# Turning six experts' token tiles by DMA: 16-bit planes stored by ScalarE and DMA transposes, for TensorE transposes

## The chip, the cores and the metric

The kernel runs on one core of a Trainium2 chip, alone. A core has engines that work from their own instruction queues: TensorE (PE, with its weight loads PEld), VectorE (DVE), ScalarE (ACT), GpSimd (POOL) and SyncE (SP), which here only issues DMAs. The metric is the device time of one execution in microseconds; a kernel is told by the median of its runs. Numbers of parts come from one profiled execution.

## The reference

Attention with a soft cap, and then a mixture of eight experts over its output. The routing is greedy and global: the largest logits first, each token to one expert, each expert at most 448 of the 3584 tokens.

```python
scores = cap * np.tanh(scale * np.matmul(q, k.transpose(0, 1, 3, 2)) / cap)
attn = softmax(scores);  x = attn @ v                # 8 x 12 heads, 448 x 64
x = x.transpose(0, 2, 1, 3).reshape(3584, 768)
flat = (x @ w_gate).flatten()
for idx in np.argsort(-flat):                        # token idx//8, expert idx%8
    if assigned[token] >= 0 or counts[e] >= 448: continue
    assigned[token] = e; counts[e] += 1
for e in range(8):
    h = np.maximum(x[mask_e] @ w1[e], 0.0)           # 448x768 @ 768x1024
    out[mask_e] = h @ w2[e]                          # 448x1024 @ 1024x768
```

All is float32. The products of the experts are made of pairs of rounded parts (a high part and the rest), three products for one.

## The kernel before, in words

The first 370 us are attention; it writes its output x, 3584 rows of 768, to a DRAM tensor `xs`. From 380 us on the experts follow each other, p = 0 to 7 in the code (expert one to expert eight in the text).

**One expert.** The first layer `ffn1` has eight steps f of 18 matmuls (144), the second layer `ffn2` eight units u: token tiles t = 0, 1, 2 of 128 tokens with 24 matmuls each and t = 3 of 64 tokens with 16, for each half of the 768 columns (176 matmuls). After every matmul the program calls `tick()`. The count of these ticks is the program's clock: at fixed ticks it writes other work into the engines' queues. PE, ACT, DVE and POOL run what the program has written, in that order; a queue's instruction starts when the queue comes to it and its semaphores allow it.

**The tokens of the next expert.** While expert p is in its second layer, the routing (class `Routing`) ends the choice of the tokens of expert p+1: `finalise` leaves the row numbers (`idx`) and the expert's number (`ei`) at tick 39 of the second layer. At tick 40 `gather(p+1)` issues four indirect DMAs on POOL (line 782): rows of `xs`, 3 KB each, to the tile `xg`, tokens on partitions. The first layer needs x the other way round, features on partitions. `xtr(p+1, c)` does this for one of six chunks c of 128 features: four TensorE transposes (line 798) to a PSUM tile psX, then `cutx`: ACT copies the rounded high part to `xgh` (line 803), DVE subtracts for the low part `xgl` (line 804). For expert p of 1 and above the six chunks lie in units u = 5, 6, 7 (the table CP); for expert two they lie in units 6 and 7 of expert one and in the first step of its own first layer (the table CL and the work lists).

**The routing beside it.** From tick 79 of the second layer on, the routing searches thresholds for expert p+2: steps of seven comparisons, five on DVE (line 503) and two on ACT (line 500, `cmpA`), whose counts a small matmul (line 507, psR) sums up. The psR matmuls stand between the matmuls of the second layer at fixed ticks: 94, 110, 126, 139, 159. The last search is that of expert seven, so it runs beside the second layers of experts two to five and not beside those of six and seven.

**Weights.** The tiles w1r (384 KB, four buffers) and w2r (768 KB, four buffers) are loaded by SP (lines 743 and 750), whose queue runs ahead of the ticks until a buffer is not free or the expert's number is not known (line 734). ACT rounds them to high parts (line 755), POOL subtracts for the low parts (line 759): `split1` and `split2`. Each finished PSUM tile of the second layer is moved by ACT (line 861, or line 864 with a DVE addition in line 865 for t = 3), and POOL scatters the rows to the output (line 840) some units later. SP is planned by the program in attention, and in the experts' part by the framework's planner.

Of the kernel before, what the change touches and what calls it, by code (L numbers as in the profile page):

```python
# [6 lines left out]
F32=mybir.dt.float32; F32R=mybir.dt.float32r; BF16=mybir.dt.bfloat16; F16=mybir.dt.float16; I32=mybir.dt.int32; I16=mybir.dt.int16  # L7
AF=mybir.ActivationFunctionType; ALU=mybir.AluOpType; AX=mybir.AxisListType
# [323 lines left out]
class Routing:  # L332
# [266 lines left out]
    def finalise(s,wp,L,update):  # L599
# [49 lines left out]
        s.results.append((idx,s.ei))  # L649
        yield 1  # L650
        if update:
          with s.tc.issue_after(mark.ins) if s.cur==0 else nullcontext():
            z=wp.tile([112,1],F32,name="zz")
            v.tensor_scalar(z,oi[:,0,0,0:1],0.0,None,op0=ALU.mult)
# [25 lines left out]


W1B=4; W2B=4
def ffn_all(nc, tc, ctx, rt, xs, w1, w2, out, ident, E, wp, deferred, xctx, gen):
# [11 lines left out]
    def units(n):  # L695
        for _ in range(n):
            if deferred: late.append(deferred.pop(0)())
    def posts():
        while late: late.pop(0)()
    N0=1; UN=[1,2,1,2,0,2,2,1,2,2,0,2,2,2,0,0]  # L700
    ctx.enter_context(tc.manual_schedule(engines={ET.PE,ET.Activation,ET.DVE,ET.Pool}))
    with tc.issue_after(rt.mark[0].ins):
        units(1)
    posts()
    m=0
    wu=[None]; end=[-99]
# [64 lines left out]
    CP=[[int(y) if y!='-' else None for y in x] for x in ',,,,,-01,2-3,45'.split(',')]  # L771
    CL=[[]]*6+[[None,None,0],[1,2]]
    def newx(p):
        if p not in xgT: xgT[p]=(fp.tile([128,DC,C],F32R,name="xgh"),fp.tile([128,DC,C],F32R,name="xgl"))
    xgp=fp.tile([128,4*DM],F32,name="xg")
    nc.gpsimd.memset(xgp[64:128,3*DM:],0.0)
    def gather(p):
        if p>=E or p in xgs: return
        need(p)
        t=xgs[p]=xgp  # L780
        for j,(o,n) in enumerate(TS):
            g=nc.gpsimd.indirect_dma_start(out=t[:n,j*DM:(j+1)*DM],out_offset=None,in_=xs,in_offset=bass.IndirectOffsetOnAxis(ap=res[p][0][:n,j:j+1],axis=0))  # L782
        return g
    def tx(p,n):
        newx(p)
        w=rt.psum()
        ps=[(ph.tile([128,512],F32,name="psH") if c>1 else pt.tile([128,512],F32,name="psX")) for c in range(n)]
        for j,(o,_) in enumerate(TS):
            for c in range(n): nc.tensor.transpose(ps[c][:,o:o+128],xgs[p][:,j*DM+c*128:j*DM+c*128+128],ident)
            if j<len(TS)-1: warm(WJ,w)  # L790
        for c in range(n): cutx(p,c,ps[c])
    def xtr(p,c):
        if p>=E or c is None: return
        newx(p)
        gather(p)
        ps=pt.tile([128,512],F32,name="psX")
        for j,(o,n) in enumerate(TS):
            nc.tensor.transpose(ps[:,o:o+128],xgs[p][:,j*DM+c*128:j*DM+c*128+128],ident)  # L798
        cutx(p,c,ps)
    def cutx(p,c,ps):  # L800
        h,l=xgT[p]
        src=ps[:,:C]
        nc.scalar.activation(h[:,c,:],src,AF.Copy)  # L803
        lo=nc.vector.tensor_tensor(l[:,c,:],src,h[:,c,:].bitcast(F32),op=ALU.subtract)
    pend=[]; cnt=[0]; cur=[0]; bc=[0]; BG=11
    def tick(n=1):
        cnt[0]+=n; bc[0]+=n; now[0]+=n
        if bc[0]>=BG:
            if pend: bc[0]=0; scatter(*pend.pop(0))
        if len(res)>cur[0]+1 and cur[0]+1 not in xgs: bc[0]=0; gather(cur[0]+1)  # L810
        if cnt[0]>=hint[0]:
            cnt[0]=0; step()
    hh={}
# [52 lines left out]
    need(0)  # L866
    WG=3; NW=12; WJ=4
    for i in range(WG): load1(0,i)
    mk=gather(0)
    with tc.issue_after(mk.ins):  # L870
        tok=xgp[0:1,2*DM:2*DM+1]
        for i in range(WG,W1B): load1(0,i,tok)
        load2(0,0,tok)
        load2(0,1,tok)
    warm(NW)
    step(); step()
    step()
# [5 lines left out]
    for p in range(E):  # L883
        lastp=p==E-1; cur[0]=p
        for f in range(FC):
            if f==0: load2(p,2)
            if f+W1B-1<FC and (p==0 or f+W1B-1>=W1B): load1(p,f+W1B-1) if (p,1,f+W1B-1) not in raw else None
            if f==2: load2(p,3)
            work={}
            if f+2<FC and (p,1,f+2) not in spl: work[3]=[lambda: split1(p,f+2)]  # L890
            at={0:[(11,0,0)],1:[(11,0,1)],2:[(11,0,2)],3:[(11,1,0)],4:[(11,0,3)],5:[(11,1,1)],6:[(11,1,2)],7:[(11,1,3)]}
            if p==0: at={1:[(11,0,0)],2:[(11,0,1)],3:[(11,0,2)],4:[(11,0,3)],5:[(11,1,0)],6:[(3,1,1),(11,1,2)],7:[(3,1,3)]}
            for n,hf,i in at.get(f,()): work[n]=[lambda hf=hf,i=i: split2(p,hf,i)]
            if p==1 and f==0: work[1]=[lambda: xtr(1,4)]; work[4]=[lambda: xtr(1,5)]
            ffn1(p,f,work)
        if lastp:
            while pend: scatter(*pend.pop(0))
            ih=f2.tile([128,2],I32,name="ih")
            for k in range(2): nc.gpsimd.tensor_scalar(ih[:,k:k+1],res[p][0][:,2:3],2.0,float(k),op0=ALU.mult,op1=ALU.add)
            nc.gpsimd.drain()  # L900
            lp[0]=False
            out2=out.rearrange("n (q d) -> (n q) d",q=2)
            for t,hf in [(t,hf) for t in (3,0,1,2) for hf in range(2)]:
                ffn2(p,t,hf,[])
                if t==2: put(out2,ih[:,hf:hf+1],ons[p][0][:,t*DM+hf*HD:t*DM+hf*HD+HD])
                elif hf==1: scatter(p,t)
            break
        for u in range(8):
            if u==4: load1(p+1,0); load1(p+1,1)
            if u==5: load1(p+1,2); load2(p+1,0)  # L910
            if u==6: load1(p+1,3)
            if u==7: load2(p+1,1)
            wk={5:{14:[lambda: split1(p+1,0)]},6:{8:[lambda: split1(p+1,1)]}}.get(u,{})
            if p<1 and u==7: wk={15:[lambda: xtr(1,3)]}
            ffn2(p,u%4,u//4,(CL if p<1 else CP)[u],wk)
            if u>3: pend.append((p,u%4))


def full(nc,tc,q,k,v,cap,wg,w1,w2,out):
    with ExitStack() as ctx:  # L920
        cp=ctx.enter_context(tc.tile_pool(name="cp",bufs=1))
        dr=ctx.enter_context(tc.tile_pool(name="dr",bufs=1,space=bass.MemoryType.DRAM))
        xs=dr.tile([3584,768],F32,name="xs")
        NDEF=4
        xd=dr.tile([2 if NDEF<4 else NDEF-2,128,6,448],F32,name="xd")
        ident=cp.tile([128,128],F32,name="ident"); make_identity(nc,ident)
        L1=cp.tile([112,32,8],F32,name="L1")
        r=Routing(nc,cp,3584,8); r.ident=ident; r.tc=tc
        xctx=ExitStack()
        xp=xctx.enter_context(tc.tile_pool(name="xp",bufs=2,side="right"))  # L930
# [16 lines left out]
        ffn_all(nc,tc,ctx,r,xs,w1,w2,out,ident,8,wp,deferred,xctx,r.phases(wp,L1,turned))  # L947


_INS=["q","k","v","cap","moe_w_gate","moe_w1","moe_w2"]  # L950
# [24 lines left out]
```

## Time and profile before

| | |
|---|---|
| median of 3 runs | 905.17 us (905.12 to 906.51) |
| the profiled execution's own time | 906.85 us |
| its span, first to last instruction | 905.1 us |
| mean granted TensorE clock | 0.995 |
| PE, DVE, ACT, POOL busy | 97%, 67%, 62%, 39% of the span |
| DMA | 123.09 MB, mean 136 GB/s |

A row of busy time by stretches gives start and end of the stretch, its length, then for each engine busy time and count, the granted clock, the DMA engines' share and GB/s. A timeline row gives start, duration of one piece, engine, line, operation, output and inputs, count, and in brackets the idle time before it with what ended it. A group's row gives busy time, mean ns of one, and idle time before. A DMA row ends with the median us from issue to landing.

### The profile page before, as it was taken

What the parts mean: (1) busy time and instruction counts of PE and PEld (TensorE: products, weight loads), DVE (VectorE), ACT (ScalarE), POOL (GpSimd) and SP (SyncE); (2) the same over time, 40 slices, a digit from 0 to 9 for tenths busy, and PEclk for the clock granted to TensorE, in tenths of its full rate; (3) what the DMA queues carried; (4) which work ended last, traced back from release to release, by engine and by line L of the source; (5) the groups of instructions that cost most, each with busy time, mean ns of one, the idle gap of its engine ahead of it and who ended that gap; (6) DMA issues with size and microseconds to landing.
All of it is one profiled execution on the core that took longest, in us unless ns stands there. A gap on an engine that the chain in (4) does not pass through costs nothing.

```text
span 905.1 us, 17559 instructions
## 1 busy us (share of the span) xinstructions
PE 876.5 (97%) x6320; PEld 643.3 (71%) x6320; DVE 604.0 (67%) x2004; ACT 564.0 (62%) x844; POOL 349.9 (39%) x501
## 2 busy tenths in 40 slices
PE   6899999999999997799999999999999999999997
PEld 3333444444333345789989989989999999999997
DVE  3688988989888888766776776767767764231210
ACT  6998898889899948273582672762752752532521
POOL 8100000000000009482593492592682773754841
PEclk9999999999999999999999999999999999999999
DMA  8799999997994017741915616407407407416301
GB/s 117 113 136 140 128 171 173 139 164 120 198 175 72 1 58 246 248 157 45 313 45 171 196 36 226 157 19 236 150 18 253 149 3 251 149 55 236 112 10 53
DMA packets 291704, 123.09 MB, mean 136 GB/s; under 512 B 224768, under 2 KB 275712, under 8 KB 291104
## 3 DMA queue, kind: packets, MB, share of 16 engines
q1 hardware_dynamic: 285104, 99.70, 49.9%
q0 software_dynamic: 4656, 22.02, 6.8%
q8 instruction: 50, 0.82, 0.4%
q10 hardware_dynamic: 1856, 0.23, 0.2%
q14 instruction: 38, 0.31, 0.1%
HBM read 97.15 MB, written 24.77 MB: 135 GB/s over the span
## 4 chain that ended last, share of the span: by engine, by line
PE 72%; issue 12%; POOL 5%; DVE 5%; SPq 3%; DMA 1%; ACT 1%; POOLq 0%; ACTq 0%; DVEq 0%
PE psH L827 20%; PE psH L855 18%; PE psA L189 12%; PE psS L148 10%; PE psM L206 4%; SPq L92 2%; PE psS L153 2%; POOL w1l L759 2%; PE psX L798 2%; PE psM L37 1%; POOL out_dram L840 1%; POOL w2l L759 1%; DVE es L165 1%; POOL xg L782 1%; DVE cmpD L503 1%
## 5 line engine op out<-in xcount | busy, mean ns | idle before, releaser
L855 PE MATMUL psH<-w2h,hh 128*128 128x384 f32 x896 | 247.0, 342 | 0.0
L855 PE MATMUL psH<-w2l,hh 128*128 128x384 f32 x512 | 175.0, 342 | 0.0
L154 ACT ACTIVATE e<-psS 128x896 f32<-128x896 f32 x168 | 147.6, 909 | 31.3 <-PE psS L148 18.7
L855 PEld LDWEIGHTS psH<-w2h,hh 128*128 128x128 f32 x896 | 162.3, 189 | 0.2
L159 ACT ACTIVATE e<-e,bias 128x1792 f32<-128x1792 f32 (+2 forms) x74 | 147.3, 1991 | 2.0
L827 PE MATMUL psH<-xgh,w1h 128*128 128x448 f32 x384 | 143.4, 373 | 0.3 <-ACT xgh L803 0.3
L827 PE MATMUL psH<-xgh,w1l 128*128 128x448 f32 x384 | 141.6, 369 | 0.0
L827 PE MATMUL psH<-xgl,w1h 128*128 128x448 f32 x384 | 141.2, 368 | 0.0
L148 PE MATMUL psS<-tq,tk 64*64 64x448 f32 x1152 | 130.9, 548 | 7.4 <-DVE tq L133 3.4
L759 POOL TENSOR_TENSOR w1l<-w1r,w1h 128x768 fp32r<-128x768 f32 x62 | 114.2, 1843 | 28.6 <-ACT w1h L755 22.5
L189 PE MATMUL psA<-e,nv 64*64 64x448 f32 x1104 | 120.9, 541 | 1.2 <-DVE xT L199 1.2
L759 POOL TENSOR_TENSOR w2l<-w2r,w2h 128x768 fp32r<-128x768 f32 x64 | 118.1, 1846 | 9.0 <-ACT w2h L755 8.7
L459 POOL TENSOR_SCALAR r_Bt<-r_b 112x4 f16<-112x4 int32 x1 | 0.2, 199 | 303.7 <-DVE rin L243 303.7
L165 DVE TENSOR_TENSOR es<-es,e 64x896 f32<-64x896 f32 (+2 forms) x74 | 100.4, 1356 | 2.7 <-ACT e L159 1.3
L835 DVE SCALAR_TENSOR_TENSOR hh<-psH,hh 128x64 fp32r<-128x64 f32 (+1 forms) x128 | 44.1, 386 | 81.2 <-ACT hh L833 79.7
L861 ACT ACTIVATE on<-psH 128x384 f32<-128x384 f32 x48 | 23.6, 491 | 119.6 <-PE psH L855 119.6
L855 PEld LDWEIGHTS psH<-w2l,hh 128*128 128x128 f32 x512 | 96.5, 189 | 0.0
L148 PEld LDWEIGHTS psS<-tq,tk 64*64 64x64 f32 x1152 | 43.7, 133 | 73.9 <-issue 40.7
L189 PEld LDWEIGHTS psA<-e,nv 64*64 64x64 f32 x1104 | 46.5, 134 | 59.9 <-issue 50.5
L833 ACT ACTIVATE hh<-psH 128x448 fp32r<-128x448 f32 x64 | 34.8, 544 | 73.2 <-PE psH L827 61.1
L827 PEld LDWEIGHTS psH<-xgh,w1h 128*128 128x128 f32 x384 | 72.5, 189 | 5.9 <-ACT xgh L803 0.5
L827 PEld LDWEIGHTS psH<-xgh,w1l 128*128 128x128 f32 x384 | 72.3, 188 | 5.7
(334 smaller groups left out, 1320.6 us busy)
## 6 DMA issues: line engine op xcount, KB each, us to landing
w1r<-in_moe_w_dram SPq DMA_DIRECT2D x64, 384.0 KB, 3.9
w2r<-in_moe_w_dram SPq DMA_DIRECT2D x32, 768.0 KB, 8.0
k<-in_k_dram SPq DMA_DIRECT2D x92, 112.0 KB, 3.4
q<-in_q_dram SPq DMA_DIRECT2D x92, 112.0 KB, 4.0
nv<-in_v_dram SPq DMA_DIRECT2D x72, 128.0 KB, 3.9
xs<-xn SPq DMA_DIRECT2D x4, 1344.0 KB, 7.4
xs<-xn SPq DMA_DIRECT2D x4, 896.0 KB, 5.1
xd<-xT SPq DMA_DIRECT2D x2, 1344.0 KB, 7.0
```

The source lines that it names most:

```text
L148: for c in range(2): nc.tensor.matmul(ps[c*64:c*64+64,h,:S],tks[g,0][hp,o,u*128+c*64:u*128+c*64+64],tks[g,1][hp,o,:],start=True,stop=True)
L154: nc.scalar.activation(ev(g,r),ps[:,:,:S],AF.Tanh,scale=sr[0])
L159: act=lambda: nc.scalar.activation(e,e,AF.Exp,scale=sr[1],bias=bias)
L165: t=es_t[g]; add=lambda o,a,b: nc.vector.tensor_tensor(o,a,b,op=ALU.add)
L189: nc.tensor.matmul(avp[g,o][h*64:h*64+64,:S],lhs,rhs[hp,h,:],start=(j==0 and x==0),stop=j==3)
L206: nc.tensor.matmul(ps[g*32:g*32+32,:S],lhs,rhs,start=first,stop=last)
L759: (eng or nc.gpsimd).tensor_tensor(view(l),r,view(h).bitcast(F32),op=ALU.subtract)
L827: nc.tensor.matmul(ps[:,:C],a[:,c,:],b[:,c,:],start=(m==0),stop=(m==DC*3-1)); m+=1
L833: nc.scalar.activation(h[:,:C],ps[:,:C],AF.Relu)
L835: nc.vector.scalar_tensor_tensor(h[:,d:d+b-a],ps[:,a:b],0.0,h[:,a:b].bitcast(F32),op0=ALU.max,op1=ALU.subtract)
L855: nc.tensor.matmul(ps[:,:HD],h[:,f,a:a+128],spl[p,2,hf,f//2][w][:,f%2,:],start=(m==0),stop=(m==nm-1))
L861: if t<3: nc.scalar.activation(ons[p][0][:,t*DM+hf*HD:t*DM+hf*HD+HD],ps[:,:HD],AF.Copy)
```

## The change

For experts three to eight the transposes of TensorE go. Instead, after the gather has landed:

- `planes(j)`, for the four token tiles j, at ticks 80, 89, 98 and 107 of the second layer: one ACT copy takes the gathered row tile as 16-bit words and separates low and high halves (two planes of 768 words), into `pl`, a tile with two buffers; ACT itself issues the store to a DRAM tensor `xz[k]`, in which the two planes of a token are neighbouring rows.
- After tiles 1 and 3, one DMA transpose on SP turns `xz[k]` (512 x 768 words, then 384 x 768) back into the gather's tile: there each partition is a feature, and the two halves of a token lie side by side, a float32 again.
- `cutt(p, k, c0, c1)`: ACT rounds three chunks of 256 or 192 tokens to the high part, DVE subtracts; four times for each expert, at ticks 156, 161, 166 and 171.
- The gather's tile is two tiles, one for each group of 256 and 192 tokens.
- The first two weight loads of the next expert are issued right behind the gather and wait for its third part (a tiny POOL copy into the tile that they fill). All other loads of the next expert stand behind the transposes in SP's queue, which the program now orders by itself here too.

```diff
-    ctx.enter_context(tc.manual_schedule(engines={ET.PE,ET.Activation,ET.DVE,ET.Pool}))
-    with tc.issue_after(rt.mark[0].ins):
-        units(1)
+    ctx.enter_context(tc.manual_schedule(engines={ET.PE,ET.Activation,ET.DVE,ET.Pool,ET.SP}))
+    units(1)
...
-    xgp=fp.tile([128,4*DM],F32,name="xg")
-    nc.gpsimd.memset(xgp[64:128,3*DM:],0.0)
+    xgp=[fp.tile([128,2*DM],F32,name=f"xg{k}") for k in range(2)]
+    row=lambda j,n=128: xgp[j//2][:n,j%2*DM:(j%2+1)*DM]
+    nc.gpsimd.memset(xgp[1][64:128,DM:],0.0)
...
+    TD=40; TJ=9; xq=[]
+    def planes(j):
+        o,n=TS[j]; k,r=divmod(j,2)
+        pl=fp.tile([128,2,DM],I16,name="pl",bufs=2)
+        nc.scalar.activation(pl[:n],row(j,n).bitcast(I16).rearrange("p (d h) -> p h d",h=2),AF.Copy)
+        nc.scalar.dma_start(xz[k][r*256:r*256+2*n].rearrange("(p h) d -> p h d",h=2),pl[:n])
+        if r:
+            n=o+n-2*128*k
+            nc.sync.dma_start_transpose(xgp[k][:,:DC*n].bitcast(I16).rearrange("p (c t) -> p c t",c=DC),xz[k])
+    def cutt(p,k,c0,c1):
+        newx(p)
+        o,n=((0,256),(256,192))[k]
+        h,l=(t[:,c0:c1,o:o+n] for t in xgT[p])
+        x=xgp[k][:,c0*n:c1*n].rearrange("p (c t) -> p c t",c=c1-c0)
+        nc.scalar.activation(h,x,AF.Copy)
+        nc.vector.tensor_tensor(l,x,h.bitcast(F32),op=ALU.subtract)
...
-        if len(res)>cur[0]+1 and cur[0]+1 not in xgs: bc[0]=0; gather(cur[0]+1)
+        if len(res)>cur[0]+1 and cur[0]+1 not in xgs:
+            bc[0]=0; n=cur[0]+1; gather(n)
+            if n>1:
+                for i in range(2): load1(n,i,xgp[1][0:1,0:1])
+                xq.extend((now[0]+TD+TJ*j,lambda j=j: planes(j)) for j in range(4))
+        while xq and xq[0][0]<=now[0]: xq.pop(0)[1]()
...
-            if u==4: load1(p+1,0); load1(p+1,1)
+            if u==4 and p<1: load1(p+1,0); load1(p+1,1)
...
-            ffn2(p,u%4,u//4,(CL if p<1 else CP)[u],wk)
+            if p and not lastp:
+                for m,k,c in {6:[(20,0,0)],7:[(1,0,3),(6,1,0),(11,1,3)]}.get(u,()): wk[m]=wk.get(m,[])+[lambda k=k,c=c: cutt(p+1,k,c,c+3)]
+            ffn2(p,u%4,u//4,CL[u] if p<1 else [],wk)
...
+        xz=[dr.tile([n,768],I16,name=f"xz{i}") for i,n in enumerate((512,384))]
```

Left out of the diff: uses of the split tile (`row(j)` in place of a slice of `xgp`), the argument `xz`, and three places where an explicit order for the framework's planner is dropped.

More of the change, by code (lines that the diff above doesn't have):

```diff
@@ L651, in finalise @@
         if update:
-          with s.tc.issue_after(mark.ins) if s.cur==0 else nullcontext():
+          if True:
             z=wp.tile([112,1],F32,name="zz")
@@ L682, with ffn_all @@
 W1B=4; W2B=4
-def ffn_all(nc, tc, ctx, rt, xs, w1, w2, out, ident, E, wp, deferred, xctx, gen):
+def ffn_all(nc, tc, ctx, rt, xs, xz, w1, w2, out, ident, E, wp, deferred, xctx, gen):
     C=448; DM=768; DC=6; DF=1024; FC=8; HD=384
@@ L770, in ffn_all @@
     xgs={}; xgT={}
-    CP=[[int(y) if y!='-' else None for y in x] for x in ',,,,,-01,2-3,45'.split(',')]
     CL=[[]]*6+[[None,None,0],[1,2]]
@@ L779, in gather @@
         need(p)
-        t=xgs[p]=xgp
+        xgs[p]=1
         for j,(o,n) in enumerate(TS):
-            g=nc.gpsimd.indirect_dma_start(out=t[:n,j*DM:(j+1)*DM],out_offset=None,in_=xs,in_offset=bass.IndirectOffsetOnAxis(ap=res[p][0][:n,j:j+1],axis=0))
+            g=nc.gpsimd.indirect_dma_start(out=row(j,n),out_offset=None,in_=xs,in_offset=bass.IndirectOffsetOnAxis(ap=res[p][0][:n,j:j+1],axis=0))
         return g
@@ L788, in tx @@
         for j,(o,_) in enumerate(TS):
-            for c in range(n): nc.tensor.transpose(ps[c][:,o:o+128],xgs[p][:,j*DM+c*128:j*DM+c*128+128],ident)
+            for c in range(n): nc.tensor.transpose(ps[c][:,o:o+128],row(j)[:,c*128:c*128+128],ident)
             if j<len(TS)-1: warm(WJ,w)
@@ L797, in xtr @@
         for j,(o,n) in enumerate(TS):
-            nc.tensor.transpose(ps[:,o:o+128],xgs[p][:,j*DM+c*128:j*DM+c*128+128],ident)
+            nc.tensor.transpose(ps[:,o:o+128],row(j)[:,c*128:c*128+128],ident)
         cutx(p,c,ps)
+    TD=40; TJ=9; xq=[]
[14 more added lines that the diff above has]
+        nc.vector.tensor_tensor(l,x,h.bitcast(F32),op=ALU.subtract)
     def cutx(p,c,ps):
@@ L868, in ffn_all @@
     for i in range(WG): load1(0,i)
[L869 to L874, printed above, removed]
+    gather(0)
+    tok=xgp[1][0:1,0:1]
+    for i in range(WG,W1B): load1(0,i,tok)
+    load2(0,0,tok)
+    load2(0,1,tok)
     warm(NW)
@@ L946, in full @@
         deferred=[lambda f=f: f((px,xr)) for f in deferred]
-        ffn_all(nc,tc,ctx,r,xs,w1,w2,out,ident,8,wp,deferred,xctx,r.phases(wp,L1,turned))
+        ffn_all(nc,tc,ctx,r,xs,xz,w1,w2,out,ident,8,wp,deferred,xctx,r.phases(wp,L1,turned))
 _INS=["q","k","v","cap","moe_w_gate","moe_w1","moe_w2"]
```

## The prediction

> **What bounds the kernel now.** I read the page first, for the busy shares; then busy time by stretches, one stretch to each expert's second layer; then the timeline of TensorE (PE) and of ScalarE (ACT) in one such stretch. Page:
>
> ```profile
> span 905.1 us, 17559 instructions
> PE 876.5 (97%) x6320; PEld 643.3 (71%) x6320; DVE 604.0 (67%) x2004; ACT 564.0 (62%) x844; POOL 349.9 (39%) x501
> PE 72%; issue 12%; POOL 5%; DVE 5%; SPq 3%; DMA 1%; ACT 1%; POOLq 0%; ACTq 0%; DVEq 0%
> ```
>
> The other engines have slack on average, but an average hides the stretch that matters. Next the second layers of experts four, six and eight (counted from one): PE alone, then only the transposes of line 798.
>
> ```profile
> 611.61:646.72 35.11, 35.11 (x219) 1.00 0.65 214
> 742.32:776.34 34.02, 34.02 (x208) 1.00 0.67 219
> 869.87:900.37 30.50, 30.50 (x177) 1.00 0.12 40
> ```
> ```profile
> 611.61:646.72 35.11, 3.59 (x24) 3.00 (x24) 1.00 0.65 214
> 869.87:900.37 30.50, 0.00 (x0) 0.00 (x0) 1.00 0.12 40
> ```
>
> PE is busy for all of every stretch: there it is the bound, and each instruction taken from it shortens the kernel unless something new makes it wait. The last expert has 176 matmuls in 30.50 us, 0.173 us each, and no transposes; the others carry 24. Four of the rows below are the routing matmuls psR, which wait for comparisons on ACT and DVE.
>
> ```profile
> 628.90 0.18 PE L507 MATMUL psR<-r_cd,r_bo 128*128 128x4 bf16 x1
> ...
> 631.99 0.18 PE L507 MATMUL psR<-r_ce,r_bo 128*128 128x8 bf16 x1
> ...
> 634.56 0.60 PE L798 MATMUL psX<-ident,xg 128*128 128x128 f32 x4
> ...
> 635.36 0.18 PE L507 MATMUL psR<-r_ce,r_bo 128*128 128x8 bf16 x1
> ...
> 636.54 0.60 PE L798 MATMUL psX<-ident,xg 128*128 128x128 f32 x4
> 636.89 0.42 PE L855 MATMUL psH<-w2l,hh 128*128 128x384 f32 x1
> 637.15 0.52 PE L855 MATMUL psH<-w2h,hh 128*128 128x384 f32 x2
> ...
> 646.72 0.36 PE L827 MATMUL psH<-xgh,w1h 128*128 128x448 f32 x1
> ```
>
> **What is removed.** From 636.54 to 637.15 stand four transposes and one matmul: 0.61 - 0.173 = 0.44 us for a group of four. Six groups are 2.65 us for each expert, and six experts (three to eight) lose them: **15.9 us** of PE. No work hides behind them, so all of it counts. The six ACT and six DVE evictions of psX go too; four cuts of wider pieces replace them.
>
> **What ACT gets.** Four copies of 1536 elements for each expert, each followed by a store that ACT issues itself.
>
> ```profile
> L159 ACT ACTIVATE e<-e,bias 128x1792 f32<-128x1792 f32 x48 | 85.9, 1790 | 1.2
> L159 ACT ACTIVATE e<-e,bias 128x2688 f32<-128x2688 f32 x23 | 58.3, 2536 | 0.7
> L755 ACT ACTIVATE w1h<-w1r 128x768 fp32r<-128x768 f32 x64 | 53.5, 836 | 9.4 <-DMA w1r<-in_moe_w_dram 9.4
> ```
> ```profile
> 0.74 1.00 ACTq L92 DMA_DIRECT2D k<-in_k_dram  x2
> ```
> ```profile
> 617.51 0.37 SPq L743 DMA_DIRECT2D w1r<-in_moe_w_dram  x1
> ```
>
> An element more costs (2536-1790)/896 = 0.83 ns, so a copy takes 836 + 768 x 0.83 = 1.48 us. No 16-bit copy of this size is in the trace: at half the rate per element it would be 0.84 us, and I keep 1.48 because the 252-element 16-bit comparison (0.51 us below) is no cheaper per element. The store waits for its copy and then holds ACT for the issue: 0.37 us (a weight load on SyncE) to 0.50 us (ACT's own two at the start); I take 0.40. One plane step is **1.88 us**. ACT runs in program order, and now stands, in order: the eviction of the third unit, planes 0, one comparison, y, planes 1, two comparisons, planes 2, planes 3, the fifth unit's eviction, two comparisons. The old times:
>
> ```profile
> 625.08 0.49 ACT L861 ACTIVATE on<-psH 128x384 f32<-128x384 f32 x1 [3.67 <-PE psH L855]
> 626.90 0.51 ACT L500 ACTIVATE cmpA<-r_VAt,r_T8A 128x252 bf16<-128x252 f16 x1 [1.33 <-DVE r_VAt L482]
> ...
> 628.05 0.49 ACT L864 ACTIVATE y<-psH 64x384 f32<-64x384 f32 x1 [0.55 <-PE psH L855]
> 629.66 0.51 ACT L500 ACTIVATE cmpA<-r_VAt,r_H8A 128x252 bf16<-128x252 f16 x1 [1.12 <-DVE r_H8A L515]
> ...
> 630.71 0.19 ACT L500 ACTIVATION_READ_ACCUMULATOR cmpA<-r_VAt,r_H8A 128x1 bf16 x1
> ...
> 633.05 0.50 ACT L500 ACTIVATE cmpA<-r_VAt,r_H8A 128x252 bf16<-128x252 f16 x1
> ```
>
> A pair of comparisons takes 630.90-629.66 = 1.24 us, one 0.63. Planes 0 needs its gather: gathers start at 619.93, the last at 624.07, and land in 4.4 us at best; they will now have the queues nearly to themselves, because the first two loads of the next expert wait for the third gather and the rest stand behind the transposes. So 624.3 to 628.5, each ahead of its copy.
>
> ```profile
> 619.93 0.98 POOL L782 DMA_INDIRECT xg<-xs,idx  x1 [8.55 <-DVE zz L654]
> ...
> 624.07 1.13 POOL L782 DMA_INDIRECT xg<-xs,idx  x1 [0.30 <-issue]
> ```
> ```profile
> DMA to landing us min/median/max: 4.4/8.0/9.2
> ```
>
> ACT then: planes 0 625.57-627.45, comparison to 628.08, y to 628.57, planes 1 to 630.45, pair to 631.69 (its psR is at 631.99: no stall), planes 2 to 633.57, planes 3 to 635.45, eviction to 635.94, pair to 637.18. The psR at 635.36 comes 0.44 us earlier once the group ahead of it is gone: 634.92. PE waits for the pair until 637.2: a **new stall of 2.3 us**. Behind that psR stands everything else of PE. It exists where a selection runs beside the second layer: experts two to five, 4 x 2.3 = 9.2 us. Bounds: steps at 2.0 us give 2.8 us, steps at 1.2 us give none.
>
> **Stores and transposes.** No DMA transpose is in the trace; the nearest rows are plain loads of like size in a quiet stretch (635 to 655 us), and small-run loads of the page:
>
> ```profile
> w1r<-in_moe_w_dram SPq DMA_DIRECT2D x3, 384.0 KB, 3.4
> w2r<-in_moe_w_dram SPq DMA_DIRECT2D x1, 768.0 KB, 6.7
> ```
> ```profile
> k<-in_k_dram SPq DMA_DIRECT2D x92, 112.0 KB, 3.4
> ...
> k<-in_k_dram SPq DMA_DIRECT2D x6, 56.0 KB, 2.4
> ...
> wgs<-in_moe_w_gate_dram SPq DMA_DIRECT2D x6, 4.0 KB, 2.0
> ```
>
> A store of 384 KB: 3.4 us; the last one (64 tokens, 192 KB): 2.9, between 2.4 and 3.4. The first transpose moves 768 KB: 6.7; the second 576 KB: 5.05, half way. Lower bound for it 3.4 (the 384 KB row); upper bound by the 128-byte runs of k: (3.4-2.0) us for 112 KB is 12.5 us for each MB, 7.2+2.0 = 9.2 us. I take 5.05 because planes are stored in long rows like those of w2r. By the Trainium skill (DMA: Bandwidth & Descriptors, section on latency and other measured facts) a DMA transpose moved 261 GB/s in one kernel; an estimate from it and the 2.0 us of the wgs row is 4.3 us for the second transpose, and the sum below would be some 1.5 us lower; no run here shows it yet.
>
> With a selection: store 3 issued at 635.05, landed 637.95, second transpose landed 643.0. The next first layer starts at 646.72-2.65+2.3 = 646.4; before its second matmul stand one ACT cut of 576 elements (0.68), one DVE subtraction (about 0.75) and two hand-overs, so the landing is due 1.5 us ahead, 644.9: in time. Without a selection (experts six and seven):
>
> ```profile
> 755.80 0.49 ACT L861 ACTIVATE on<-psH 128x384 f32<-128x384 f32 x1 [3.67 <-PE psH L855]
> 758.57 0.49 ACT L864 ACTIVATE y<-psH 64x384 f32<-64x384 f32 x1 [2.28 <-PE psH L855]
> ```
>
> Here the two plane buffers decide: planes 0 756.29-758.17, y to 759.06, planes 1 to 760.94; planes 2 waits for store 0 (757.77+3.4 = 761.17) and ends at 763.05, planes 3 for store 1 (763.94), its store issued 765.42, landed 768.32, transposed 773.37. Due: 776.34-2.65-1.5 = 772.2 (776.34 is the end of the stretch in the second fence). Late by **1.2 us**, twice 2.4.
>
> What costs nothing: the two tiny GpSimd copies that hold the first loads wait for the third gather (627.1), with nothing behind them on GpSimd but the scatter after the fifth unit's eviction. SyncE's wait on the stores delays the other loads of the next expert to about 639; after the transposes they need about 9 us (3 MB at the 359 GB/s or less of the busy stretch before), and each is used 1 to 4 us after it lands; without that margin it would be up to 1 us for each expert. The cuts (0.84 and 0.68 us twice) take ACT about as long as the six evictions they replace.
>
> **Sum**: -15.9 + 9.2 + 2.4 = -4.3 us, with 891 and 918 as the ends below. The profiled execution took 906.85 us around its 905.1 us span, 1.7 above the median of the runs; taken from that median, 905.17, it is **901**.
>
> **Rivals.** *ACT holds less than I price* (chance 0.20). Half-rate copies bring a step to 1.24 us; then neither stall is left and nearly all 15.9 us stay: 889 to 893, say 891. For it: a 2-byte copy is not in the trace. Against: the comparison rows.
>
> *The stall lowers PE's clock* (0.18). The trace shows it:
>
> ```profile
> 373.52:376.93 3.41, 1.43 (x13) 1.00 0.92 311
> 376.93:380.34 3.41, 3.41 (x19) 0.50 0.30 94
> ```
>
> A stretch in which PE was busy 1.43 of 3.41 us is followed by 3.41 us at half clock, 1.7 us lost. A 2.3 us stall inside one such stretch leaves PE busy for 1.1. If all four stalls do it: 901 + 4 x 1.7 = 908. If a stall falls across two stretches, nothing. The Trainium skill (TensorE: Matmul & The Clock Gate, Part 1) lets the clock fall after an idle window of about 3.4 us; by that rule 2.3 us would do no harm, but the rows show that a partly busy window was enough.
>
> *The transposes are late and hold ACT* (0.20), the other side. A cut that waits on ACT has the evictions behind it, and PE the first layer. Both transposes carry 4.7+3.05 us of data by the rows above; from 1.2 times that on, the second lands too late with a selection too. At 1.5 times: 633.45 (store 1) + 2 + 11.6 = 647.1, 2.2 late, four times 8.8; without a selection 763.94 + 13.6 = 777.5, 5.3 late, twice 10.7. -15.9+9.2+8.8+10.7 = +12.8: **918**. At 2.2 times, the k rows' bound, some 946. For it: two-byte elements turned; against: rows of 1.5 KB at the source.
>
> **How the numbers follow.** Forecast 0.38 (898 to 904.5), cheap ACT 0.20, clock 0.18, late transposes 0.20; 0.04 for mishaps with the weight loads. The range 890 to 918 leaves out the tail of late transposes and a full gain. A measurement of this kernel tells about 0.2% (1.8 us) from no change. Faster: 0.38 x 0.7 + 0.20 + 0.01 = 0.48; same: 0.38 x 0.3 + 0.05 of the clock case = 0.16; slower 0.36.
>
> **What would show it.** No L798 group after 460 us. ACT back to back from the third unit's eviction to the pair before the third psR, and PE idle some 2 us before that psR, in four stretches: the stall; no idle there, and it was ACT's price. PE clock 0.5 just after: the clock. ACT waiting for a DMA at the cuts, with the transposes' times to landing above 6 us: the transposes. PE busy throughout with shorter stretches would refute the forecast.

## The result, and the profile after

The changed kernel takes **929.81 us** (median of 4 runs, 928.75 to 930.77) where the kernel before takes 905.50 (905.12 to 906.51) beside it: ratio 1.0266, interval 1.0249 to 1.0284. It is 24.3 us slower; 901 was forecast, at most 918. The page of the profiled execution, lines on span, busy time and the chain that ended last:

```profile
span 928.4 us, 17350 instructions
PE 873.8 (94%) x6176; PEld 638.1 (69%) x6176; DVE 606.6 (65%) x1992; ACT 594.9 (64%) x856; POOL 352.6 (38%) x513
PE 75%; DVE 7%; DMA 7%; ACT 4%; issue 3%; SPq 2%; POOL 0%; ACTq 0%; POOLq 0%; DVEq 0%
```

The chain now goes through DMA for 7% of the span, where it was 1%. PE's busy time fell by 2.7 us only, though 15.9 us of transposes are gone: something else made its matmuls longer. The second layers of experts four, six and eight again, PE by stretches (busy, granted clock, DMA share, GB/s):

```profile
616.97:654.18 37.21, 34.28 (x195) 0.95 0.65 192
756.64:792.74 36.10, 31.47 (x184) 0.97 0.61 175
893.14:923.60 30.46, 30.46 (x177) 1.00 0.12 39
```

The eighth, which turns nothing, takes what it took. The fourth has 24 matmuls fewer and takes 2.1 us more: PE is idle for 2.9 us of it, and its clock is below full. The groups of PE from 485 to 930 us name the waits (last columns: idle time, and what ended it); before, all three had 0.0.

```profile
L847 PE MATMUL psH<-xgh,w1h 128*128 128x448 f32 x288 | 110.0, 382 | 10.5 <-ACT xgh L813 10.5
L847 PE MATMUL psH<-xgl,w1h 128*128 128x448 f32 x288 | 109.2, 379 | 4.3 <-DVE xgl L814 4.2
L507 PE MATMUL psR<-r_ce,r_bo 128*128 128x8 bf16 x32 | 5.7, 178 | 10.7 <-ACT cmpA L500 10.2 <-DVE cmpD L503 0.3
```

These are 25.5 us of waiting, of three kinds. The third row is the forecast stall at the third psR of four experts. The first is the late transpose, 4.63 us ahead of expert seven's first layer and 5.22 ahead of expert eight's. The second is a wait for the low parts. Beside them stands the clock. The records give the granted clock for windows of 3.41 us. PE in such windows, each beside the one that follows it (the granted clock is the figure behind the bracket), and then the sum over all seven half-clock stretches from 507 us to 866 us, two of them two windows long:

```profile
640.64:644.05 3.41, 0.90 (x6) 1.00 1.12 265
644.05:647.46 3.41, 3.41 (x13) 0.50 0.69 197
...
582.61:586.02 3.41, 1.86 (x9) 1.00 1.05 346
586.02:589.43 3.41, 3.41 (x11) 0.50 1.03 407
...
572.37:575.78 3.41, 1.82 (x11) 1.00 1.18 305
575.78:579.19 3.41, 3.41 (x22) 1.00 0.69 158
...
sum 30.70, PE 26.06; mean PE 3.72
```

PE worked 26.06 us at half clock, so **13.0 us** of it is lost. -15.9 + 25.5 + 13.0 = +22.6 us; the spans differ by 23.3. The third pair is the end of the stall beside expert three's second layer: it fell across two windows, and the clock stayed full behind a window in which PE was busy for 1.82 us, hardly less than the 1.86 of the second pair. So these records give no single busy share at which the clock falls.

How the stall comes about shows in ACT's timeline beside expert four's second layer, and PE's row behind it:

```profile
630.45 0.49 ACT L881 ACTIVATE on<-psH 128x384 f32<-128x384 f32 x1 [3.67 <-PE psH L875]
630.84 1.48 ACT L803 ACTIVATE pl<-xg 128x1536 int16<-128x1536 int16 x1
632.34 0.34 ACTq L804 DMA_DIRECT2D xz<-pl  x1
...
639.46 1.49 ACT L803 ACTIVATE pl<-xg 64x1536 int16<-64x1536 int16 x1 [1.15 <-DMA xz<-pl]
640.97 0.47 ACTq L804 DMA_DIRECT2D xz<-pl  x1
641.49 0.49 ACT L881 ACTIVATE on<-psH 128x384 f32<-128x384 f32 x1 [0.55 <-ACT pl L803]
641.88 0.50 ACT L500 ACTIVATE cmpA<-r_VAt,r_H8A 128x252 bf16<-128x252 f16 x1
...
642.50 0.50 ACT L500 ACTIVATE cmpA<-r_VAt,r_H8A 128x252 bf16<-128x252 f16 x1
```
```profile
643.15 0.17 PE L507 MATMUL psR<-r_ce,r_bo 128*128 128x8 bf16 x1 [2.71 <-ACT cmpA L500]
```

A copy takes 1.48 us and its issue 0.34 to 0.47, about as priced (1.48 and 0.40). Only the 1.15 us in which planes 3 waits for its buffer, that is for store 1, was not foreseen here.

How the transposes come late: issue and landing of store 3, of the first and of the second transpose beside the same layer, each asked for by itself.

```profile
L804 ACTq DMA_DIRECT2D xz<-pl x1: 473/473/473, 641.0 to 641.0; - x1
DMA to landing us min/median/max: 3.8/3.8/3.8
...
L807 SPq DMA_TRANSPOSE xg<-xz x1: 3092/3092/3092, 639.5 to 639.5; - x1
DMA to landing us min/median/max: 5.6/5.6/5.6
...
L807 SPq DMA_TRANSPOSE xg<-xz x1: 2487/2487/2487, 644.9 to 644.9; - x1
DMA to landing us min/median/max: 5.2/5.2/5.2
```

Store 3 and the first transpose land together, at 644.8 and 645.0, and the second transpose is issued there. The queues' packets from 640.8 to 643.9 us say what ran meanwhile (q1 carries SP's transfers, q10 ACT's stores):

```profile
q1 hardware_dynamic: 3061, 0.78, 112.7%
q10 hardware_dynamic: 22, 0.07, 6.2%
```

In 3.1 us the transpose moved 3061 packets and the store 22. In all six experts the second transpose is issued at most 0.2 us before the first one lands.

### The profile page after: what moved, and what is told of

It is laid out like the page before. It is cut to its first block, busy times and chain, and to the rows that moved or that the text cites. A ratio compares the mean times of both kernels' runs of the same rounds, so it can differ in the third digit from the quotient of the medians.

```text
span 928.4 us, 17350 instructions
## 1 busy us (share of the span) xinstructions
PE 873.8 (94%) x6176; PEld 638.1 (69%) x6176; DVE 606.6 (65%) x1992; ACT 594.9 (64%) x856; POOL 352.6 (38%) x513
## 4 chain that ended last, share of the span: by engine, by line
PE 75%; DVE 7%; DMA 7%; ACT 4%; issue 3%; SPq 2%; POOL 0%; ACTq 0%; POOLq 0%; DVEq 0%
PE psH L847 26%; PE psH L875 18%; PE psA L189 11%; PE psS L148 10%; PE psM L206 3%; DMA xg<-xz 3%; DMA xz<-pl 3%; DVE cmpD L503 2%; SPq L92 2%; PE psS L153 2%; ACT pl L803 2%; DVE es L165 1%; PE psM L37 1%; DVE xgl L814 1%; DMA k<-in_k_dram 1%
## 5 line engine op out<-in xcount | busy, mean ns | idle before, releaser
L875 PEld LDWEIGHTS psH<-w2h,hh 128*128 128x128 f32 x896 | 165.3, 192 | 2.6 <-issue 2.4
L847 PE MATMUL psH<-xgh,w1h 128*128 128x448 f32 x384 | 146.8, 382 | 10.8 <-ACT xgh L813 10.5
L847 PE MATMUL psH<-xgl,w1h 128*128 128x448 f32 x384 | 144.6, 377 | 4.3 <-DVE xgl L814 4.2
L847 PE MATMUL psH<-xgh,w1l 128*128 128x448 f32 x384 | 144.1, 375 | 0.0
L847 PEld LDWEIGHTS psH<-xgh,w1h 128*128 128x128 f32 x384 | 74.6, 194 | 18.2 <-ACT xgh L813 12.1
L847 PEld LDWEIGHTS psH<-xgl,w1h 128*128 128x128 f32 x384 | 74.2, 193 | 12.1 <-DVE xgl L814 6.4
```

Source lines behind the costliest of these rows:

```text
L847: nc.tensor.matmul(ps[:,:C],a[:,c,:],b[:,c,:],start=(m==0),stop=(m==DC*3-1)); m+=1
L875: nc.tensor.matmul(ps[:,:HD],h[:,f,a:a+128],spl[p,2,hf,f//2][w][:,f%2,:],start=(m==0),stop=(m==nm-1))
```

## The experiments

All times are medians; the kernel before had 905.5 to 906.3 beside them.

**The copies made short.**

```diff
-        pl=fp.tile([128,2,DM],I16,name="pl",bufs=2)
-        nc.scalar.activation(pl[:n],row(j,n).bitcast(I16).rearrange("p (d h) -> p h d",h=2),AF.Copy)
+        pl=plc[j%2]
+        nc.scalar.activation(pl[:n,:,0:1],row(j,n).bitcast(I16).rearrange("p (d h) -> p h d",h=2)[:,:,0:1],AF.Copy)
```

Left out of the diff: `plc`, two tiles filled once with a constant, in place of the two buffers of `pl`.

> The copy of a plane step takes two elements instead of 1536; the rest of the planes that are stored is a constant, so the tokens of experts three to eight are not the right ones. Stores, transposes, cuts and all waits stay. Theory A (ScalarE's four copies hold the routing's comparisons and delay the stores; from that come the waits of TensorE and from those the half clock): a step falls from 1.82 to about 0.55 us, the 2.5 us waits at the third psR go, the second transpose lands 4 us earlier, no wait at the first layers, clock 1.0 throughout: 888 to 893 us. Theory T (the transposes are too slow in themselves, 5 to 8 us each): TensorE still waits 3 to 5 us ahead of the first layers of experts seven and eight, with half clock behind: 900 to 910 us.

Measured: 929.66 us (924.51 to 932.18), ratio 1.0271 (1.0251 to 1.0291): no gain, and far above both expected ranges. PE's groups from 485 us on, in the profiled execution (924.51 us, the fastest of the four):

```profile
L849 PE MATMUL psH<-xgh,w1h 128*128 128x448 f32 x288 | 110.2, 383 | 14.3 <-ACT xgh L815 14.3
...
L507 PE MATMUL psR<-r_ce,r_bo 128*128 128x8 bf16 x32 | 5.8, 183 | 2.6 <-ACT cmpA L500 2.5
```

The stall at psR fell from 10.7 to 2.6 us, so the copies do cause most of it; but the wait for the transposed x rose from 10.5 to 14.3. Beside expert four's second layer (616.97 us on in the changed kernel, 621.57 on here) the second transpose is issued 28.0 us after its start there and 27.1 here, while the next first layer starts 34.2 us after it instead of 37.2, and has still waited 1.4. The copies are not what sets the chain of transfers. Here store 3 is issued 0.1 to 0.2 us behind the first transpose (1.5 in the changed kernel) and lands while that still runs, so the second transpose is issued 2.6 to 4.8 us before the first has landed. Yet nothing is won by it: the first now takes 7.9 to 10.1 us to land, where it took 5.6 to 5.9, and from its issue to the last landing pass 11.1 to 13.3 us, where it was 10.7 to 13.4.

**Two more plane buffers**, in weight tiles that are idle then.

```diff
-        pl=fp.tile([128,2,DM],I16,name="pl",bufs=2)
+        pl=(fp.tile([128,2,DM],I16,name="pl",bufs=2) if j<2 else ws.tile([128,DC,128],F32R,name="w1h" if j==2 else "w1l",bufs=3).rearrange("p c f -> p (c f)").bitcast(I16).rearrange("p (h d) -> p h d",h=2))
```

> The planes of the third and fourth token tile go to two other, idle tiles, so that no plane step waits for a store. Theory A: planes 3 starts 1 us earlier beside a selection and 2.4 to 3 us earlier without; the waits at the third psR fall from 2.5 to about 1.4 us (4 times), those ahead of the first layers of experts seven and eight from 4.6 and 5.2 to about 2.3 us, the 1.3 us waits for xgl mostly go, and some of the half clock: 911 to 919 us. Theory T: only the psR waits fall, 923 to 926 us.

Measured: 925.73 us, ratio 1.0207 (1.0180 to 1.0234), 4 us better than the changed kernel and in the range of theory T: psR 7.6 us, but 11.0 and 4.6 in the first layers. With no wait for a buffer store 3 is issued close to the first transpose and lands 3.8 us or more later, before that transpose: the second is issued 0.5 to 4.4 us ahead of the first one's landing, and the first takes 7.2 to 8.4 us. As with the short copies, the transfers share their time and end no earlier.

**The two early weight loads ahead of the gather.**

```diff
-            bc[0]=0; n=cur[0]+1; gather(n)
-            if n>1:
-                for i in range(2): load1(n,i,xgp[1][0:1,0:1])
+            bc[0]=0; n=cur[0]+1
+            if n>1:
+                for i in range(2): load1(n,i)
+            gather(n)
+            if n>1:
```

> The first two weight loads of the next expert are written ahead of the gather and wait for nothing but the expert's number, so that they have landed before the gather starts. Theory A with collisions (store 1 takes 4 to 5 us instead of 3 because it shares the DMA engines with these loads): store 1 lands 1 to 1.5 us earlier, psR waits 1 us shorter (4 times), the two long waits 1.5 us shorter, some half clock less: 915 to 922 us. If the collision is not what delays store 1: 927 to 930 us.

Measured: 919.96 us, ratio 1.0170 (1.0136 to 1.0205), as expected: without these loads beside it store 1 lands 2.3 us after its issue, where it took 3.9 to 4.9, and the waits ahead of the last two first layers fall to 1.8 us each. Still the second transpose is issued about when the first lands (1.0 us before it beside expert four, at most 0.3 elsewhere).

**Dummy matmuls where PE waits**: ahead of the third psR, ahead of the first layer of experts seven and eight, and behind the first matmul of it for experts four to six. First 20, 40 and 12 of them, then 11, 20 and 6.

```diff
+            if s.cur>2 and ab=="A" and i==2: s.warm(20,s.pp.tile([128,512],F32,name="psX"))
...
+        if f==0 and p>5: warm(40,pt.tile([128,512],F32,name="psX"))
...
+            if m==1 and f==0 and 2<p<6: warm(12,pt.tile([128,512],F32,name="psX"))
```

> Dummy matmuls on the identity (0.11 us each) stand where TensorE waits: 20 ahead of the third psR for experts two to five, 12 behind the first matmul of the first layers of experts four to six, 40 ahead of the first layers of experts seven and eight. They compute nothing that is used. Theory A: the waits stay as they are but the clock stays at 1.0, and some 11 to 13 us of half clock come back: 915 to 919 us. If the half clock has another cause than the idle time: 928 us or slower.

> The changed kernel with dummy matmuls in the places where the tensor engine waits: 11 ahead of the third psR of experts two to five's searches, 6 behind the first matmul of the first layer for the fourth, fifth and sixth expert, 20 ahead of the first layer of the seventh and eighth (0.227 us each by the row of the run with more of them: 2.5, 1.4 and 4.5 us, the lengths of the waits). If the half clock after each wait is a cost of its own of 11 to 13 us: 917 to 920 us, with no half-clock window after 500 us. If the clock in the records is only a sign of the waits: 928 to 932.

Measured: 935.16 us, ratio 1.0321 (1.0303 to 1.0338), with the larger numbers; 922.25 us, ratio 1.0168 (1.0137 to 1.0199), with the smaller, between its two ranges. The first lies in the range of another cause of the half clock, but for a different reason: a dummy as written is two matmuls and takes 0.227 us, twice what that run assumed (timeline of the first run, groups of the second):

```profile
790.92 9.09 PE L711 MATMUL psX<-ident 128*128 128x128 f32 x80
```
```profile
L850 PE MATMUL psH<-xgh,w1h 128*128 128x448 f32 x288 | 107.1, 372 | 2.8 <-ACT xgh L814 2.8
L850 PE MATMUL psH<-xgl,w1h 128*128 128x448 f32 x288 | 106.3, 369 | 0.6 <-DVE xgl L815 0.6
L711 PE MATMUL psX<-ident 128*128 128x128 f32 x204 | 24.2, 275 | 0.0
```

In neither is a half-clock window left between 500 us and the end, and the first layer's matmuls are back at some 370 ns. In the second, 102 dummies are 23.2 us; with 3.4 us of waits left in these rows and 1.5 at psR, PE waits or runs dummies for 28.1 us, 2.6 more than the 25.5 of the changed kernel, and yet it is 7.6 us faster: the half clock is worth 10.2 us. In the first, 196 dummies and 1.3 us of waits make 45.8, 20.3 more, for 5.4 us more: 14.9. These lie on either side of the 13.0 of the records. The clock is a cost of its own.

**No first transpose.**

```diff
-            nc.sync.dma_start_transpose(xgp[k][:,:DC*n].bitcast(I16).rearrange("p (c t) -> p c t",c=DC),xz[k])
+            if k: nc.sync.dma_start_transpose(xgp[k][:,:DC*n].bitcast(I16).rearrange("p (c t) -> p c t",c=DC),xz[k])
```

> The first DMA transpose of each expert is left out, so tokens 0 to 255 of experts three to eight stay unturned (the output is wrong there); copies, stores, the second transpose and all cuts stay. Theory A (whatever is issued while a transpose runs lands only at its end): store 3 lands within 3 us of its issue instead of 3.8 to 5.6, the second transpose is issued 3 to 5 us earlier, the waits of 4.6 and 5.2 us ahead of experts seven and eight and most of their half-clock windows go: 911 to 916 us. The stalls at the third psR of 2.3 to 2.7 us stay, as the copies are still there. Theory B (stores are slow because of the weight loads, or by themselves): store 3 still lands 3.8 us or more after its issue, the second transpose comes 1 us earlier at most, 924 to 928 us.

Measured: 920.73 us, ratio 1.0159 (1.0142 to 1.0176). The time lies between the two ranges: five of the nine half-clock windows stay, three behind the third psR and two behind the waits for the low parts. For store 3 it is as theory A says, not B. The remaining transpose is issued 2.7 us behind store 3 (median of six; 4.2 in the changed kernel), and the waits for xgh fall to 1.9 us:

```profile
L847 PE MATMUL psH<-xgh,w1h 128*128 128x448 f32 x288 | 108.2, 376 | 1.9 <-ACT xgh L813 1.9
L847 PE MATMUL psH<-xgl,w1h 128*128 128x448 f32 x288 | 107.5, 373 | 5.4 <-DVE xgl L814 5.4
```

**Both transposes behind the last store**, in two tries; the second has the order of the diff's loop and of the cuts turned round.

```diff
-        if r:
-            n=o+n-2*128*k
-            nc.sync.dma_start_transpose(xgp[k][:,:DC*n].bitcast(I16).rearrange("p (c t) -> p c t",c=DC),xz[k])
+        if j==3:
+            for k,n in ((0,256),(1,192)): nc.sync.dma_start_transpose(xgp[k][:,:DC*n].bitcast(I16).rearrange("p (c t) -> p c t",c=DC),xz[k])
```

> The changed kernel with both DMA transposes of an expert issued one behind the other, after the fourth store. Theory A (a store that is issued beside a transpose waits for its end): store 3 now lands within 3 us, 2.7 as in the run without the first transpose, since no transpose runs by then. If the two transposes then run one after the other, 5.6 and 5.2 us, the last lands 13.5 us behind the issue of store 3 (9.5 in the changed kernel), and each of the six first layers starts 3 to 4 us later: 940 to 955. If they overlap, the second lands some 3 us behind the first, 11 us behind store 3, 1.5 us later than now: 931 to 938. Theory B (store 3 is slow without a transpose too): it lands 3.8 us or more after its issue here as well.

> The changed kernel with both DMA transposes of an expert issued behind the fourth store: the second first, as it waits for that store and SP runs in order, and the cuts in that order too. Theory A (a store issued beside a transpose lands only with its end): the first of the two transposes is issued 2.8 us or less behind the issue of store 3 (it was 4.0 and more). If the two then run one after the other, the last lands 13.5 us behind the issue of store 3 (9.5 in the changed kernel): each of the six first layers starts 3 to 4 us later, 940 to 955. If they overlap, 11 us, 931 to 938. Theory B (store 3 is slow without a transpose too): the first is issued 3.8 us or more behind the issue of store 3.

Measured, first try: 930.97 us, ratio 1.0276 (1.0261 to 1.0291). It does not separate the theories: the first transpose waits for its own two stores only, and went out as early as before. Second try: 938.94 us, ratio 1.0369 (1.0350 to 1.0388), and with no transpose running store 3 lands in 2.6 to 2.7 us in all six experts, where it took 3.8 to 4.2. Beside expert four's second layer:

```profile
L804 ACTq DMA_DIRECT2D xz<-pl x1: 473/473/473, 645.3 to 645.3; - x1
DMA to landing us min/median/max: 2.6/2.6/2.6
```

So what slows store 3 is the transpose beside it, not its own size. That it lands only with the transpose's end, as theory A has it, is so in the changed kernel but not in general: with short copies and with four buffers it landed before. Issued one behind the other, the two transposes need 8.9 to 10.5 us together, 4.8 to 6.2 to the first landing; in the changed kernel they took 5.6 and 5.2 beside expert four, 10.8 together: here they overlap by 2 us at most. The last lands 11.7 to 13.3 us behind the issue of store 3, and the time, too, lies between the two expectations.

**Half of the tokens left on PE**: tokens 256 to 447 turned by PE into three PSUM tiles of two chunks, tokens 0 to 255 by planes and one transpose, the early loads ahead of the gather. First with the last tile 64 wide (`row(3,64)` by `ident[:64,:64]`), then with whole tiles, as in the diff, and earlier cuts.

```diff
...
+        for i in range(2):
+            for j in range(2): nc.tensor.transpose(ps[:,i*256+j*128:i*256+j*128+128],row(2+j)[:,(c+i)*128:(c+i)*128+128],ident)
...
-                xq.extend((now[0]+TD+TJ*j,lambda j=j: planes(j)) for j in range(4))
+                xq.extend((now[0]+TD+TJ*j,lambda j=j: planes(j)) for j in range(2))
...
```

> Only tokens 0 to 255 go by planes and one DMA transpose; tokens 256 to 447 are turned by the tensor engine, 12 transposes an expert into three psX tiles of two chunks, each evicted at once; the two early weight loads go ahead of the gather. Theory A (the serial chain of two transposes, and four copies in ScalarE's queue, cost the time): no wait for the cuts and none at the third psR, so 6 x (2.65 - 1.33) = 7.9 us below before, 897 to 899. Theory B (any DMA transpose in this stretch delays the weight loads or the scatters enough to be felt): 903 to 910.

> Only tokens 0 to 255 go by planes and one DMA transpose; tokens 256 to 447 are turned by the tensor engine, now in whole 128 by 128 tiles (the last tile's padding is zero), three groups of four an expert, and the cuts of the transposed half come 5 steps earlier; the first two weight loads go ahead of the gather. If the run before it with 64-wide tiles lost its gain to the change of tile shape (0.99 us a group there, 0.445 for a group of four whole tiles in the kernel before) and to cuts that came 0.5 us late: 6 x (2.65 - 1.33) = 7.9 us below before, 897 to 900. If one DMA transpose an expert by itself costs what it saves: 904 to 908.

Measured, with the 64-wide tile: 910.11 us, ratio 1.0043 (1.0026 to 1.0059), at the edge of theory B's range, but with no PE wait worth a row except 1.9 us for the low parts. Its timeline shows where the gain went, beside that of the version with whole tiles:

```profile
570.35 0.52 PE L887 MATMUL psH<-w2h,hh 128*128 128x384 f32 x2
570.71 0.27 PE L803 MATMUL psX<-ident,xg 128*128 128x128 f32 x1
570.91 0.28 PE L804 MATMUL psX<-ident,xg 64*128 64x64 f32 x1
571.11 0.33 PE L803 MATMUL psX<-ident,xg 128*128 128x128 f32 x1
571.37 0.27 PE L804 MATMUL psX<-ident,xg 64*128 64x64 f32 x1
571.57 0.45 PE L887 MATMUL psH<-w2l,hh 128*128 128x384 f32 x1
571.86 0.51 PE L887 MATMUL psH<-w2h,hh 128*128 128x384 f32 x2
```
```profile
570.44 0.34 PE L886 MATMUL psH<-w2h,hh 128*128 128x384 f32 x1
570.62 0.60 PE L803 MATMUL psX<-ident,xg 128*128 128x128 f32 x4
570.97 0.42 PE L886 MATMUL psH<-w2h,hh 128*128 128x384 f32 x1
571.23 0.34 PE L886 MATMUL psH<-w2l,hh 128*128 128x384 f32 x1
```

With shapes in turn, a group of four takes 571.86 - 570.52 (570.35 and one matmul) less two matmuls of 0.173, 0.99 us; whole tiles take 571.23 - 570.44 less the same, 0.44. Three groups at 0.99 are more than the six that were removed. With whole tiles: **898.95 us**, ratio 0.9923 (0.9911 to 0.9935), in the range expected if the tile shape and the late cuts had cost the first version its gain, and faster than both kernels, with 2.1 us of waits at psR left and nothing else.

**What that gain is not**: all turning on PE, with the rest of the change, and then with the early loads ahead of the gather too.

```diff
-                xq.extend((now[0]+TD+TJ*j,lambda j=j: planes(j)) for j in range(4))
...
+            ffn2(p,u%4,u//4,(CL if p<1 else CP)[u],wk)
```

> The changed kernel without planes, DMA transposes and cuts: all experts are turned by the tensor engine where the kernel before did it; what stays of the change is SP in the written order, the gate tile cut in two, and the first two weight loads asked for at the gather. If the rest of the change costs nothing: 904 to 908, no wait of the tensor engine over 0.5 us behind 480 us. If the early loads or the order of SP cost by themselves: 910 or more.

> All experts turned by the tensor engine as in the kernel before, with the first two weight loads put ahead of the gather as in the run that turned half the tokens there. If the gain of that run is the transposes it takes off the tensor engine: 904 to 907 here, no change. If it is the earlier loads: 898 to 901.

Measured: 906.31 us, ratio 1.0001 (0.9992 to 1.0010), and 906.14, ratio 0.9999 (0.9989 to 1.0009), with no PE wait worth a row. The order of SP, the cut gather tile and the earlier loads cost and bring nothing; the loss of the change is all in planes, transposes and cuts, and the gain of the half version is the transposes that it takes off PE.

**One transpose for three tiles**, the last 64 tokens on PE; then with the copies begun earlier and the cuts in four pieces.

```diff
-        if r:
-            n=o+n-2*128*k
-            nc.sync.dma_start_transpose(xgp[k][:,:DC*n].bitcast(I16).rearrange("p (c t) -> p c t",c=DC),xz[k])
+        if j==2:
+            nc.sync.dma_start_transpose(xgp[0].bitcast(I16).rearrange("p (c t) -> p c t",c=DC),xz[0])
...
```

> Tokens 0 to 383 go by planes and a single DMA transpose of 768 rows; the last 64 tokens are turned by the tensor engine, six transposes into one psX tile; the two early weight loads go ahead of the gather. Theory A (the chain is serial, so one transpose in place of two ends it 4 to 6 us earlier): 6 x (2.65 - 0.5) = 12.9 us less transposing, with stalls of about 1.5 us at the third psR in four experts, 6 us, and half a window of clock at each, 7 us: 893 to 905. Theory B (a transpose of three tiles takes as long as the two together, and lands late ahead of experts seven and eight): 908 to 915.

> Tokens 0 to 383 by planes and a single DMA transpose, as in the run before, with the three copies begun 4 steps earlier and 8 steps apart, and the cuts in four pieces, the first of one chunk. The waits of that run (5.0 us for xgh, 2.8 for xgl, 1.6 at psR, two half-clock windows) should fall to 3 us in all if they came from when the steps stand: 898 to 903. If the single transpose, 9 us from issue to landing, is what sets it: 907 to 912.

Measured: 910.81 us, ratio 1.0052 (1.0035 to 1.0069), and 910.56, ratio 1.0046 (1.0032 to 1.0060), both in the range that blames the single transpose. In the first PE waits 5.0 us for xgh and 2.8 for xgl. In the second these are 0.9 together, so the transpose is no longer what PE waits for; but the comparisons now stand behind the copies on ACT and the cuts' subtractions on DVE: 8.0 and 3.6 us at the two kinds of psR. The waits moved from one place to the other.

## Why the prediction was wrong, point by point

**What is removed (15.9 us): right.** The version with half the groups was worked out at 7.9 us and brings 6.6, with 2.1 us of new waits; leaving all groups on PE changes nothing.

**What ACT gets: the cause right, the size in part by luck.** The stall was put at 2.3 us four times and measured 2.3 to 2.7; short copies left 0.5 to 1.2 of it. But with four buffers it was 1.6 to 2.0: the copies were priced somewhat too high, and the wait of planes 3 for a slow store, which the prediction did not have beside a selection, made up for it.

**Stores and transposes: the first step that failed.** It let store 3 land after 2.9 us and the second transpose begin then, at 637.95, though the first, by the same step's figures, would have run from 633.45 to 640.15: two transfers that share the queues' engines were timed each as if alone. In the kernel the store lands with the first transpose, the second starts there, and the lateness of 1.2 us ahead of experts seven and eight became 4.63 and 5.22. Ahead of expert seven two parts can be told apart. Store 1, which shares its time with the two early weight loads, was issued at 774.8 and took 4.9 us where 3.4 was said (2.3 without the loads); and from its landing to that of the second transpose passed 12.3 us, where the step had 9.4. The transposes' own sizes matter less: beside expert four the first took 5.6 us where 6.7 was said, the second 5.2 where 5.05 was. The estimate from the Trainium skill (DMA: Bandwidth & Descriptors, latency and other measured facts), 4.3 us from its 261 GB/s, is below every landing in the changed kernel (5.2 to 7.7 us).

The rival of late transposes had 5.3 us without a selection, close to what came, but by transposes that are slower themselves, and 2.2 us four times with a selection, where PE waited at most 0.2 us for xgh. Its number for experts seven and eight is near by luck. (Its tail, at 2.2 times, gives 950 us by its own terms, not 946.)

**A queue that was not read.** Before the first layer's second matmul the step counted one cut and one subtraction. On DVE five comparisons of the search stand ahead of that subtraction. DVE, and PE behind it, at the start of expert five's first layer:

```profile
653.35 0.44 DVE L503 TENSOR_SCALAR_CACHE_REDUCE cmpD<-r_qt,th 128x224 bf16<-128x224 f16 x1
...
655.18 1.42 DVE L814 TENSOR_TENSOR xgl<-xg,xgh 128x576 fp32r<-128x576 f32 x2
```
```profile
655.98 0.47 PE L847 MATMUL psH<-xgl,w1h 128*128 128x448 f32 x1 [1.33 <-DVE xgl L814]
```

The second transpose had landed at 650.1 and ACT's first cut of its tokens ended at about 654.1; a subtraction of one such piece takes some 0.7 us, so about 1 us of the 1.33 is the order of DVE's queue. Three such waits are 4.0 us. Without the first transpose they were as long; no run removed these comparisons by themselves.

**The clock: the second step that failed, and the larger.** The sum has no term for it; as a rival it was given 0.18 and 6.8 us, for the four stalls alone. It came with three of the four (the fourth fell across two windows, the case for which the rival said nothing is lost), with both late transposes, and with two of the three waits of 1.33 us: 13.0 us by the records, 10.2 and 14.9 by the two runs that kept PE busy. The row of the prediction (1.43 of 3.41 us busy, then half clock) already said that a partly busy window can be enough; a window busy for 1.86 was, too, and one busy for 1.82 was not. What decides between these two stays open. The Trainium skill (TensorE: Matmul & The Clock Gate, Part 1) has the clock fall after an idle window; by that rule, read as a window without any work, none of these waits would have cost more than itself, and the trace disagrees.

By its own sum: -4.3, with the late transposes 7.5 us more (9.9 for 2.4), the waits for xgl 4.2, the clock 13.0 and the stall 1.0, is +21.4, against a difference of the spans of 23.3. Some 2 us stay unexplained.

## What to carry to other kernels

When PE is busy throughout, a wait costs itself and, in most places here, the half clock behind it: price both, and lay the other engines' queues out beside every hand-over, not only the engine that got the new work. Transfers that run together share their time: a store, loads and transposes that fall into the same few microseconds are timed one after the other, and where a trace shows that they overlap, each is longer. A partial version (here half of the tokens by DMA, where nothing waits) can gain where the whole loses.

## What was not expected of the hardware

- In the changed kernel a store issued 1.5 us behind a DMA transpose lands some 0.2 us before the transpose does: 3.8 to 4.2 us, against 2.6 to 2.7 with none running. Records of 3.1 us hold 3061 packets of the transpose and 22 of the store. Where the store was issued closer to the transpose it landed earlier than that, and the transpose took longer: 7.2 to 10.1 us against 5.6 to 5.9.
- A DMA transpose holds SP's queue for 2.3 to 3.5 us at its issue in the changed kernel, and lands 5.2 to 7.7 us after it.
- The clock fell to half after windows of 3.41 us in which PE was busy for 0.90 and for 1.86 us, and stayed full after one in which it was busy for 1.82.
- Transposes of 128 and 64 wide in turn cost 0.99 us a group of four, those of one shape 0.44.
